# Raw query blocks as pairs of 1024 columns, feed-forward work in half units and new hand-written orders in a fused attention and feed-forward kernel

## The chip, the cores and the metric

The kernel runs on one core of a Trainium2 chip. The metric is the device time of one execution in microseconds (us); here three runs are shown. A second number is the span of one profiled execution, from its first to its last instruction. The engines have short names in what follows: PE (TensorE, matrix multiplications), DVE (VectorE), ACT (ScalarE), POOL (GpSimd) and SP (SyncE, which here only issues transfers). PSUM is the accumulator memory, eight banks of 512 f32 columns on 128 partitions.

## The reference

```python
# S = 2048 tokens, D = 448, H = 16 heads of 28, F = 1792, all float32
g = sigmoid((x * gate_w).sum(-1, keepdims=True))
qkv = (x @ wqkv).reshape(B, S, 3, H, 28)
p = softmax(q @ k.T * 28 ** -0.5)          # per head
a = (p @ v) @ wo
gate = x @ W_gate
h = gate * (gate > 0) * (x @ W_up)
b = h @ W_down
out = g * a + (1 - g) * b
```

## The kernel before

There are three phases. The first, up to about 140 us, makes Q, K and V with three-pass high and low products and writes Q and K to DRAM (`qk_d`). The last, from 1017 us, is the down projection and the output projection. Between them lie **32 rounds**. Round r works on head h = r // 2 and on eight of its sixteen key tiles, against all 2048 queries, which are four blocks of 512 (0 to 3).

What PE, ACT and DVE issue inside a round, and in which order, is written out by hand in the list of strings `ROUNDS`, one string per round. A letter is one piece of work, and the digit behind it is the PSUM bank it uses:

- **m**: a row maximum (`smax`). PE multiplies 128 queries by 512 keys (L288) of a head that comes *later*, and DVE reduces the bank to one column (L290). When all maxima of a head are there, `smax_end` writes the maxima as extra rows of that head's Q, so that scores come out already lessened by the maximum. The list `MAXIMA` runs over the heads in order, so an m belongs to whichever head is next in that list, wherever it stands.
- **s**: a score tile (`scores`). PE multiplies 128 keys by 512 queries (L315), and ACT writes its exponential to SBUF (L317).
- **r, d, e**: the *raw* way, for a query block without row maxima. PE makes a raw score tile for the next round (`raw_scores`, L323), ACT copies it to SBUF (L327), DVE keeps a running maximum (`raw_max`, d, L330). At the end of the round `raw_top` reduces that maximum over the partitions with transposes and reductions (L340 to L353), sends the row to DRAM (`mr_d`, L354) and broadcasts it back (L357) into the one tile `top`. In the next round POOL subtracts it from each raw tile (`raw_less`, L361), and ACT takes the exponential (e, `raw_exp`, L365).
- **x**: one pass of the feed-forward gate and up products (`gu_mm`, L701). A unit has two halves of ten passes and one last pass with 64 rows; the last passes of the two halves run side by side on the two halves of PE's rows.

Before the change, block 3 goes the raw way in every round from the third, and block 2 too where `WIDE` or `BOTH` name the head; a head then has 16, 12 or 8 rows of tiles with maxima (`rows_of`, `parts_of`).

A round ends with the last feed-forward passes, `raw_exp` for what is left, `relu`, in odd rounds the loads of head h + 3's K (`load_k`, four transfers), then `raw_top`, the products `gate * up` (`spill_h`), Q (`load_q`, four transfers and a fifth from `z_d`), the next feed-forward weights (`next_w`) and last `pv`: 64 matmuls of the probabilities by V (L739). Nearly all transfers are issued on SP, one behind the other in program order; where SP waits for a transfer's input or for its buffer, those behind it wait too. K and Q have three buffers each (`h % 3`), so head h + 3 overwrites head h, whose last scores are in round 2h + 1. The maxima of head h + 3 are the first to use the new data.

Of the kernel before, what the change touches and what calls it, by code (L numbers as in the profile page):

```python
# [9 lines left out]
F32 = mybir.dt.float32  # L10
# [9 lines left out]
P = 128  # L20
S = 2048
D = 448
H = 16
# [26 lines left out]
    ("m2m3m6m7s0s1uxxxxs0xm2lxs1xm3xxs6s2xm0m7xUxxxm3m6xs2m0s7m1xxs3m2xxm7xm1m0s3s2xxm7xxm1s0xxm3m7xm1s2m0xs3xxxxm"  # L50
     "2m3xs1xm0xm2xs3xm1xm0xx"),
    ("xxr2s1m0xm3s7r6m2xxs1s3s7dm0xr2dxxxs6s1xm0s3s7xr2xm6s0xds3xs7xm6s1r2m3xs7xs6dm1r0xr3xxdm7s2s1xdxs0xs2m7s1s3x"
     "xxs2m7s0r1m3xs2xxxxdm3s0s2xxxxxs0xs3m2s1xxs0xs3s2m1"),
    ("xxr6m2r1m0xs3r7xxs2r6xxds0xr1dxs2ds7xdr3m0xs6m2xs1m7dxs0xs2m6m1s7xs0r3m2s6dxs7xxs1m2s0m6xm7r3xs1s0dxm2xxm1m7"
     "xs3xxm0s2s1xm3s7exm2s0m1xexem3xm2xxm0exm3exxm2xs1m0xxem3xm1s2m0"),
    ("xxs0m2s1m7s6xxm0s3m2r1xr7m6s0dxs2m3s1xm6s0m7r2xdr1s3xm0s6xxexds7r3m2m0s6xxs7r1xdm2s0s6xdm7s3xs2m0s1m6xs3m7s2"
     "s0m1xr6m3r7es2xs1ds0d"),
    ("xxr2m0m6r1m3r7r2xdxs1r0xs6ddxxr3m1xr7xds6xm2s0xs1dr3xm6s0em2xxr7xs6dm1xs2m0s3xds6s1m2xs3xm0s6s7m2m1xr3xs0xxd"
     "s7xs2m1r0dxs7m3s2xs1xxs7m0s2r3m1xexxdr2s0xxdxr1xxxdem3r0xdxr2dxs1"),
    ("xxs0xm7xs1m2xs3m6m7xs1s0m3xs2m6s7xxm0m1xm2s7xr6m3xs1m7s0xm2xs1s3xs7m6r2m1xs3xem0m7xxxr1xr0s3xxr7dxds2xxr1edd"  # L60
     "xxdr3xr0dxxexexxm1eedxxxxem3xm1em2x"),
    ("xs7r0r2m6s1xm7dr3xs0xm6xdr1s7m0dxr2xds6xr3xr7dxs1s0s6xxds2xm1s3xxs6m0s2m1m3s7s6xm2s0xm1s7s3m6xs2m0s1s7m3xs6m"
     "2s1em0exm3r7s6m2s1m0d"),
    ("xxm7s1r2m0r6m3xr1xm7s0xds2m3xs6xm7s1s2m0s3m6xs7m1r2m0xr3xs7xddr1xdxs0m7r6xs2s3dr0m1xs7xm2xr6ds3xxs7xdr1m2ds3"
     "s0xxm7exxs2m3s0r1m7xds2xm3r0xs7xm2s1xxr3dxdxr1s2xm0exxxr3exxr0ds2dxdx"),
    ("xxs2m7r1m0s6xr3m2s1s7m0r6xm3dr2xxds0s1m7xr3xs6xds1xm2r7dxr6s0s3xxdxm1exxm0er7m6xs1xds3xs0m2m1s6xr3m7dr0s2xex"
     "xdr1xm7dxexxr0m3r2xedxxer1xxr3xxr0exxxdxxdds2m1xde"),
    ("xxxm0m2r7s1m3xs6xm7r2m0xxdxs3m1xs6xm0m2s3xm7s1xm0r6m3s2xxdxr7m0s2dexr1xm6xs2m0m3s7dxexxs2xs7m0xm3xs1m2s7em0x"
     "xs3m1exm7m2xr0dr3dxxexxxm2r1xxxexm0m3exs2dxxe"),
    ("xxr7m1s0r6m2ds3xm7s1r0xxdr2s3xxds1xr6m7xr0xs1s2dm3xdr7xs1m6xs3xds0s2s1m6xm3s0m7xexs6m2s1m0xs3s7m6m2s1xs3m0s7"  # L70
     "s6m1xs2m3r0m7s6dm1s2e"),
    ("xxs2m0s7m1r3xm6s2m0xs7xr3m1s6m2xxs7m3r0m6s1xr2dxs7s3s6ds1xxm0xm2s7m3s6xr0m1s2m7s6s3xxs1dm2xxs6m3s0m1s2r7m6xs"
     "3xdm1xs2xr0m3r7dxxr1xxds3r2dxm0xs7dxr3r1dxxr0xr2xddexxxxedr1m3dxr0xxdxe"),
# [24 lines left out]
    ("xxr7m6r1r0xxr2xr1xs3r6ddxdxr0dr7xr2xs3xdxdr6xxr0xr1dxdr3xdds2xs7s6xxdm0s2s1m7m3exxs2m0m1r7xexxs2ds3m0xxxm1es"
     "2m7s3m0xexr1m2s3xdexxs0xm2s3exm1exm0xr3em2dxxxs1m0"),
    ("xxs0m2s7m1r3m6xs0m2xr1m7s3xm0s6m2r1r7xxdr6xs0ds3r2dxxxm7ds0xs1r6m3xs0dxr2m1ds7xs3xr0m6s1xxr2xr3dxedxxr1s0xr7"  # L100
     "xxdxes3dxdr0m1ds2xxxexm3xxm1er2m0dexm3exxr1xexxdm0ex"),
    ("xxr7m2s0m6r1m3xs7m2s0r6m1dxs7s3xm0s2xm1r7dxs3r6xr0m2xs1s3ds7dxxem2xr6m1xr3m7dxs0xdr1s2xxs7dr0xxxs2dxs7r1exm3"
     "s2xxm7r0dxdexm3exxxexr1xm2r0ddxxr3dxxexr2xdexexxm1"),
    ("xxxm0m2r7s1m3xs6xm7r2m0xxdxs3m1xs6xm0m2s3xm7s1xm0r6m3s2xxdxr7m0s2dexr1xm6xs2m0m3s7dxexxs2xs7m0xm3xs1m2s7em0x"
     "xs3m1exm7m2xr0dr3dxxexxxm2r1xxxexm0m3exs2dxxe"),
    ("xs7m2s1m6xr3s0m7s1m2xs3m6m0xs7m2r1xs3dm6xs7r0xm2s3xxdm7m1es6xr3xs0m2s6xr7xdm1s0s2xdr6m3xs1xds2m7s0xs3m1s6m2x"
     "s0m7s3xm1s6s2m0xr7m3dr6s1em2m0d"),
    ("xxs2r7s1s0xr3xdxs2s7xr6s0s1dxxs3r2xds0s7xs6r3s1xxs7xds2s0xr1s6s3xs2dxs7xs6r0s3r1dxxs7ds2exs6e"),
    ("xs7s2s0r1xr6s7xs2dxr1s0s3xs7xdxs2r0s6s3dxs7s1xr2s6xds3xxr0r1xdexxdxes6s3xs2xxs6s7s3xs0r1s2s6d"),
    ("xxs1xs0xs2s3s6xxxxs1s2s7xxs0xs6xxxxs7s1xs3xxs2s0xxxxxes2xs1s7xexes2exxs1xs3xxxs0xxxxxexexxs1s2"),  # L110
]

WIDE = (2, 4, 6, 8, 10, 12, 13)

BOTH = (4, 6, 8, 10, 12, 13)

# [12 lines left out]
def gated_mix_kernel(ctx, tc, x, wq, wo, wgu, wd, out):  # L129
# [17 lines left out]
    banks = [psum.tile([P, TB], F32, name=f"b_{k}") for k in range(8)]  # L147
# [80 lines left out]
    def raw_js(r):  # L228

        return [] if r < 2 else [3, 2] if r // 2 in (WIDE if r % 2 else BOTH) else [3]  # L230

    def raws(r):
        return [(i, j) for i in range(8 * r, 8 * r + 8) for j in raw_js(r)] if r < 2 * H else []

    def prob(i, j):
        r, k = divmod(i, 8)
        if j == 3 or j in raw_js(r):
            if j == 3 and r % 2 == 0:
                return slot(k)[:, 3]
            if j == 2 and r % 2 and r // 2 in BOTH:  # L240
                return slot(k)[:, 2]
            return V.rearrange("p g h k d -> p (g h k d)")[:, (k + 8 * (3 - j)) * TB:(k + 8 * (3 - j) + 1) * TB]
        return slot(k)[:, j]
# [4 lines left out]
    def top(a, n=1):  # L248
        return slot(8)[:, 2 + a:2 + a + n].rearrange("p a t -> p (a t)")
# [23 lines left out]
    def rows_of(h):  # L273

        return NK if h == 0 else NK - 8 if h in BOTH else NK - 4

    def parts_of(h, u):
        return 2 if h in WIDE and u > 7 else 4

    MAXIMA = [(h, u, c) for h in range(H) for u in range(rows_of(h)) for c in range(parts_of(h, u))]  # L280

    def smax(k, ps):
# [3 lines left out]
        if u == 0 and c == 0:  # L286
            MX[h] = keep.tile([P, 4 * n], F32, name=f"mx_{h}", tag="mx", bufs=2)
        nc.tensor.matmul(ps, Q[h][:, u * P:(u + 1) * P], K[h % 3][:, c * TB:(c + 1) * TB], start=True, stop=True)  # L288
        at = 4 * u + c - (2 * (u - 8) if parts_of(h, u) == 2 else 0)
        nc.vector.tensor_reduce(MX[h][:, at:at + 1], ps, axis=AX.X, op=OP.max)  # L290
        if u == n - 1 and c == parts_of(h, u) - 1:
            M[h] = keep.tile([P, n], F32, name=f"m_{h}", tag="m", bufs=2)
# [39 lines left out]
    def raw_top(r):  # L332
# [6 lines left out]
        for a in range(n):  # L339
            nc.vector.transpose(run(a), run(a))  # L340
# [763 lines left out]
```

## Time and profile before

| | |
|---|---|
| time, three runs | 1196.99, 1204.61, 1202.27 us, median 1202.27 |
| span of the profiled execution | 1198.7 us (its own time is not given) |
| first phase | 0 to about 140 us |
| rounds 0 to 31 | about 140 to 1017 us |
| last phase | 1017 to 1199 us |
| busy share of the span | PE 99%, DVE 75%, ACT 70%, POOL 52% |

The end of a round is the end of its `pv` block on PE: round 7 at 365.4, round 8 at 396.3, round 10 at 448.5, round 11 at 479.3, round 12 at 507.3, round 16 at 618.2, round 17 at 646.2, round 23 at 811.7, round 24 at 845.4. In the profile a line such as L288 is a line of the kernel; "b" is a PSUM bank, "P" and "V" hold probability tiles, "mx" the columns of maxima. A timeline row gives the start, the length and the instruction, and in brackets how long the engine had been idle ahead of it and what released it.

### The profile page before, as it was taken

How to read it: one execution, taken by the hardware profiler on the slowest of the kernel's cores; microseconds unless marked ns; L12 is line 12 of the kernel's file. 1: busy time of each engine (PE TensorE's matmuls, PEld its weight loads, DVE VectorE, ACT ScalarE, POOL GpSimd, SP SyncE). 2: the span in 40 equal slices, each digit the busy share in tenths (PEclk: the TensorE clock that was granted, in tenths of full speed). 3: DMA queues.
4: the chain of work that ended last, by engine and by line, in shares of the span. 5: the costliest groups of instructions: out<-in, count | busy, mean ns of one | idle time of the engine just before them, and what ended most of it. 6: DMA issues, size and time to landing. Idle time of an engine off the chain costs nothing. (4 is left out here: it accounts for less than half of the span.)

```text
span 1198.7 us, 18744 instructions
## 1 busy us (share of the span) xinstructions
PE 1186.6 (99%) x6343; PEld 858.2 (72%) x6343; DVE 900.3 (75%) x1579; ACT 839.4 (70%) x1671; POOL 627.4 (52%) x631
## 2 busy tenths in 40 slices
PE   9999999999999999999999999998999999999998
PEld 6888866666576666667666766666666666989998
DVE  5498777888788879888898889887888872553342
ACT  5311668798998888888888888986998886532121
POOL 4332325566875864776388557657688474100000
PEclk9999999999999999999999999999999999999999
DMA  8956755363646361644554253625452452743432
GB/s 295 340 211 243 264 183 184 114 208 97 211 142 217 128 198 55 191 122 166 182 176 159 68 169 119 200 88 179 149 178 81 160 150 84 232 147 115 132 115 83
DMA packets 68936, 195.89 MB, mean 163 GB/s; under 512 B 15170, under 2 KB 21858, under 8 KB 64414
## 3 DMA queue, kind: packets, MB, share of 16 engines
q1 hardware_dynamic: 55896, 148.72, 38.8%
q0 software_dynamic: 12512, 45.51, 10.7%
q8 instruction: 50, 0.82, 0.3%
q10 hardware_dynamic: 432, 0.46, 0.1%
q14 instruction: 46, 0.38, 0.1%
HBM read 133.99 MB, written 61.12 MB: 163 GB/s over the span
## 5 line engine op out<-in xcount | busy, mean ns | idle before, releaser
L290 DVE TENSOR_REDUCE mx<-b 128x1 f32<-128x512 f32 x680 | 441.6, 686 | 48.8 <-PE b L288 46.0
L317 ACT ACTIVATE P<-b 128x512 f32<-128x512 f32 x672 | 373.7, 633 | 65.5 <-PE b L315 62.8
L701 PE MATMUL b<-X,wg 128*128 128x512 f32 (+1 forms) x1232 | 394.1, 399 | 1.9 <-DMA wg<-wgs_d 1.6
L701 PEld LDWEIGHTS b<-X,wg 128*128 128x128 f32 (+1 forms) x1232 | 217.5, 188 | 69.4 <-issue 20.9
L288 PE MATMUL b<-K,Q 128*128 128x512 f32 x680 | 257.4, 392 | 3.8 <-DMA Q<-z_d 2.0
L315 PE MATMUL b<-Q,K 128*128 128x512 f32 x680 | 247.8, 391 | 0.0
L361 POOL TENSOR_TENSOR V<-V,P 128x512 f32<-128x512 f32 x176 | 224.8, 1294 | 32.9 <-DMA P<-mr_d 27.9
L361 POOL TENSOR_TENSOR P<-P,P 128x512 f32<-128x512 f32 x168 | 214.9, 1294 | 28.9 <-DMA P<-mr_d 15.6
L739 PE MATMUL b<-P,v 128*32 128x512 f32 x1680 | 228.5, 594 | 0.0
L330 DVE TENSOR_TENSOR P<-b,P 128x512 f32<-128x512 f32 x279 | 186.3, 684 | 12.9 <-ACT P L327 6.7
L739 PEld LDWEIGHTS b<-P,v 128*32 128x32 f32 x1680 | 68.4, 110 | 132.1 <-issue 111.8
L739 PE MATMUL b<-V,v 128*32 128x512 f32 x368 | 156.0, 594 | 0.8 <-ACT V L365 0.8
L288 PEld LDWEIGHTS b<-K,Q 128*128 128x128 f32 x680 | 127.9, 188 | 32.1 <-issue 2.4
L315 PEld LDWEIGHTS b<-Q,K 128*128 128x128 f32 x680 | 127.7, 188 | 29.6 <-ACT P L317 2.0
L1009 PE MATMUL b<-WD,hh 128*128 128x448 f32 x672 | 138.2, 366 | 0.3
L1009 PEld LDWEIGHTS b<-WD,hh 128*128 128x128 f32 x672 | 126.1, 188 | 10.9 <-DVE WD L186 0.5
L323 PE MATMUL b<-Q,K 128*128 128x512 f32 x344 | 131.8, 391 | 0.0
L327 ACT ACTIVATE V<-b 128x512 f32<-128x512 f32 x168 | 104.3, 635 | 24.0 <-PE b L323 23.5
L365 ACT ACTIVATE V<-V 128x512 f32<-128x512 f32 x176 | 110.6, 670 | 3.6 <-POOL V L361 3.5
L180 ACT ACTIVATE hh<-hr 128x512 fp32r<-128x512 f32 x52 | 32.8, 631 | 109.3 <-PE b L1009 109.3
L365 ACT ACTIVATE P<-P 128x512 f32<-128x512 f32 x168 | 105.5, 679 | 2.6 <-POOL P L361 2.6
L327 ACT ACTIVATE P<-b 128x512 f32<-128x512 f32 x160 | 98.5, 625 | 8.5 <-PE b L323 7.3
(102 smaller groups left out, 1039.7 us busy)
## 6 DMA issues: line engine op xcount, KB each, us to landing
wg<-wgs_d SPq DMA_DIRECT2D x42, 896.0 KB
Q<-qk_d SPq DMA_DIRECT2D x64, 224.0 KB
h_d<-rl POOLq DMA_DIRECT2D x56, 256.0 KB, 3.5
hr<-h_d SPq DMA_DIRECT2D x52, 256.0 KB
wgs_d<-wg SPq DMA_DIRECT2D x14, 896.0 KB
K<-qk_d SPq DMA_DIRECT2D x52, 224.0 KB
qk_d<-st POOLq DMA_DIRECT2D x21, 512.0 KB, 4.9
wgr<-wgu SPq DMA_DIRECT2D x13, 512.0 KB
```

What stands on the lines that cost most here:

```text
L288: nc.tensor.matmul(ps, Q[h][:, u * P:(u + 1) * P], K[h % 3][:, c * TB:(c + 1) * TB], start=True, stop=True)
L290: nc.vector.tensor_reduce(MX[h][:, at:at + 1], ps, axis=AX.X, op=OP.max)
L315: nc.tensor.matmul(ps, K[h % 3][:, kt * P:(kt + 1) * P], Q[h][:, j * TB:(j + 1) * TB], start=True, stop=True)
L317: nc.scalar.activation(prob(i, j), ps, AF.Exp, scale=SCALE)
L323: nc.tensor.matmul(ps, K[h % 3][:, kt * P:(kt + 1) * P], Q[h][:, j * TB:(j + 1) * TB], start=True, stop=True)
L327: nc.scalar.activation(own, ps, AF.Copy)
L330: nc.vector.tensor_tensor(run(3 - j), ps, run(3 - j) if i % 8 > 1 else prob(i - 1, j), op=OP.max)
L361: nc.gpsimd.tensor_tensor(own, own, top(3 - j), op=OP.subtract)
L365: nc.scalar.activation(own, own, AF.Exp, scale=SCALE)
L701: nc.tensor.matmul(ps, WS[i][rows, s, a], xf(i // NF, b)[rows], start=(n == 0), stop=(n == NT - 1))
L739: nc.tensor.matmul(po[32 * j:32 * j + 32], VH[h][:, i % NK], prob(i, j), start=(i == i0), stop=(i == i0 + ni - 1))
L1009: nc.tensor.matmul(ACC[i // NF][t][:, :D], HH[i][:, a, t * P:(t + 1) * P], WD[:, f, b], start=(f == 0 and n == 0), stop=(f == NF - 1 and n ...
```

## The change

It does the following.

- Query blocks 2 and 3 both go the raw way in every round from the third. They are handled as one tile of 1024 columns: two matmuls into two neighbouring banks, then one ACT copy, one running maximum, one POOL subtraction and one exponential of 1024 columns each.
- Head 0 keeps 16 rows of tiles with maxima, and each later head has 8 with four columns: 544 row maxima in all, where there were 680.
- PSUM becomes one tile of eight banks, so that a pair of banks can be read by one instruction.
- Feed-forward work is dealt out in half units: a round holds three halves (18 rounds) or four, so a unit can end in the next round. There are 1100 x letters as before. `gu_mm` still pairs the last passes by lanes, where both halves stand in one round.
- A new letter T places `raw_top` inside the order; 23 rounds have it (not 0, 1, 4, 10, 11, 14, 18, 28 and 31). There `raw_top`, with its two transfers, comes ahead of `load_k`.
- All 32 orders are new. Round 1 has no m; rounds 2 to 27 have 16 on average.
- Smaller: the raw copies of round 1 go to DVE instead of those of rounds 29 and 30; `relu` goes to DVE from round 29; V has one buffer, loaded in the head's own first round, at the sixth s; `rl` has three buffers; `load_k` is always on SP.

The core of the diff:

```diff
-WIDE = (2, 4, 6, 8, 10, 12, 13)
-
-BOTH = (4, 6, 8, 10, 12, 13)
+PASSES = 10
...
-    banks = [psum.tile([P, TB], F32, name=f"b_{k}") for k in range(8)]
+    whole = psum.tile([P, 8, TB], F32, name="b")
+    pairs = [whole[:, k:k + 2] for k in range(0, 8, 2)]
+    banks = [whole[:, k] for k in range(8)]
...
     def raws(r):
-        return [(i, j) for i in range(8 * r, 8 * r + 8) for j in raw_js(r)] if r < 2 * H else []
+        return range(8 * r, 8 * r + 8) if 2 <= r < 2 * H else []
...
     def rows_of(h):
-        return NK if h == 0 else NK - 8 if h in BOTH else NK - 4
+        return NK if h == 0 else NK - 8
...
-    def raw_scores(i, j, ps, late=False):
+    def raw_scores(i, b, late):
...
+        for j in (2, 3):
+            nc.tensor.matmul(banks[b + j - 2], K[h % 3][:, kt * P:(kt + 1) * P], Q[h][:, j * TB:(j + 1) * TB], start=True,
+                             stop=True)
+        ps = pairs[b // 2].rearrange("p a t -> p (a t)")
         if late:
-            nc.vector.tensor_copy(own, ps)
+            nc.vector.tensor_copy(prob_pair(i), ps)
         else:
-            nc.scalar.activation(own, ps, AF.Copy)
...
+    def raw_max(i, b):
+        nc.vector.tensor_tensor(run(0, 2), pairs[b // 2].rearrange("p a t -> p (a t)"),
+                                run(0, 2) if i % 8 > 1 else prob_pair(i - 1), op=OP.max)
...
+    def raw_less(i):
+        own = prob_pair(i)
+        nc.gpsimd.tensor_tensor(own, own, top(), op=OP.subtract)
...
+    HALVES = [order.count("x") // PASSES for order in ROUNDS] + [0]
+    done = sum(HALVES) // 2
...
+            elif o == "T":
+                assert not new and not tops
+                raw_top(r + 1)
+                topped = True
...
         if r % 2 and h + 3 < H:
-            load_k(h + 3, nc.gpsimd if nxt % NF == 0 else nc.sync)
+            load_k(h + 3)
         if r % 2 == 0:
             next_w()
-        if raws(r + 1) and r:
+        if not topped:
             raw_top(r + 1)
```

What this does to the order on the engines shows at three places. First, SP in the odd round 17, before: its K, Q and z loads (K_175 and Q_178 are head 11's buffers) and `raw_top`'s two transfers (`mr_d_103`, and the broadcast into P_1499).

```order
L373 DMA f_d_125<-rows_179 32x32
L376 DMA fa_5626<-f_d_125 32x512 x2
L260 DMA K_175<-qk_d 28x2048 x4
L354 DMA mr_d_103<-rows_179 16x32
L357 DMA P_1499<-mr_d_103 128x512
L266 DMA Q_178<-qk_d 28x2048 x4
L269 DMA Q_178<-z_d 2x2048
L690 DMA wg_1241<-wgs_d_138 128x1792
```

The same place on SP after the change (K_168 and Q_171 are head 11's buffers now).

```order
L358 DMA f_d_118<-rows_172 32x32
L361 DMA fa_5151<-f_d_118 32x512 x2
L340 DMA mr_d_96<-rows_172 32x32
L343 DMA P_1500<-mr_d_96 128x1024
L254 DMA K_168<-qk_d 28x2048 x4
L260 DMA Q_171<-qk_d 28x2048 x4
L263 DMA Q_171<-z_d 2x2048
L676 DMA wg_1238<-wgs_d_129 128x1792
```

`mr_d` and the broadcast moved ahead of the four K loads, which stood ahead of them before; Q follows K directly.

Second, PE at the start of round 18, behind round 17's last `pv` matmul, before: L288 is a row maximum, L315 a score, L323 a raw score, L701 a feed-forward pass. K_174 and Q_177 belong to head 10, loaded in round 15; the first use of head 11's K_175 and Q_178 stands some 40 matmuls further on.

```order
L739 MATMUL b_72<-V,v_4904 32x512
L701 MATMUL b_73<-X_166,wg_3081 128x512 x2
L323 MATMUL b_76<-Q_176,K_173 128x512
L288 MATMUL b_70<-K_174,Q_177 128x512
L315 MATMUL b_69<-Q_176,K_173 128x512
L323 MATMUL b_75<-Q_176,K_173 128x512
L288 MATMUL b_71<-K_174,Q_177 128x512
```

After the change (L725 is `pv`, L288 the transpose of head 10's finished maxima, L279 a row maximum, L302 a score):

```order
L725 MATMUL b<-V,v_4957 32x512 x2
L288 MATMUL b<-ident,m_5300 8x128
L279 MATMUL b<-K_168,Q_171 128x512
L302 MATMUL b<-Q_169,K_166 128x512
L279 MATMUL b<-K_168,Q_171 128x512
L302 MATMUL b<-Q_169,K_166 128x512
L279 MATMUL b<-K_168,Q_171 128x512
```

The first maximum of the round now uses head 11's K_168 and Q_171, which SP loads in round 17; the same holds for the first maximum of each even round from 2 to 26.

Third, DVE at the end of round 17 after the change: the last maxima, running maxima (L319) and the pieces of `raw_top` (L328 to L336).

```order
L319 TENSOR_TENSOR P_1500<-b,P_1500 128x1024
L280 TENSOR_REDUCE mx_4917<-b 128x1 x2
L319 TENSOR_TENSOR P_1500<-b,P_1500 128x1024
L328 STREAM_TRANSPOSE P_1500<-P_1500 128x512 x2
L331 TENSOR_REDUCE best_of<-P_1500 128x32
L325 TENSOR_REDUCE P_1500<-best_of 32x32 x4
L334 TENSOR_REDUCE P_1500<-P_1500 32x32
L336 STREAM_TRANSPOSE rows_172<-P_1500 32x32
L280 TENSOR_REDUCE mx_4917<-b 128x1 x2
L283 TENSOR_REDUCE m_5300<-mx_4917 128x8
```

Two row maxima and their final reduction (L283) stand behind `raw_top` now; before, `raw_top` stood behind all of the round's maxima, as the last work of DVE ahead of the feed-forward products.

More of the change, by code (lines that the diff above doesn't have):

```diff
@@ L56 @@
[L56 to L61, printed above, removed]
@@ L660, in gated_mix_kernel @@
     WSB = [fe.tile([P, 2, 7, P], F32R, name=f"wg_{k}") for k in range(2)]
-    done = sum(order.count("x") for order in ROUNDS) // 20
+    HALVES = [order.count("x") // PASSES for order in ROUNDS] + [0]
+    done = sum(HALVES) // 2
     def lane(k):
@@ L878, in gated_mix_kernel @@
                 keep_w(1)
[L879 to L880 removed]
+        assert not todo and not mine and not rest and not new, r
+        gone = made
         for i, half, ps in units:
             gu_mm(ps, i, half, NT - 1)
[L883 to L884 removed]
+        if exps:
+            raw_exp(exps.pop(0))
         for i, half, ps in units:
```

251 lines of the change are left out of this document (118 added, 133 removed).

## Prediction

> **What bounds the kernel now.** I began with the busy shares and the clock of the page.
>
> ```profile
> span 1198.7 us, 18744 instructions
> PE 1186.6 (99%) x6343; PEld 858.2 (72%) x6343; DVE 900.3 (75%) x1579; ACT 839.4 (70%) x1671; POOL 627.4 (52%) x631
> PEclk9999999999999999999999999999999999999999
> ```
>
> PE is busy for 99% of the span at full clock, so each matmul that goes is worth its slot, and each stall that comes costs all of its length. No other engine has more than 75%. Next I cut the rounds out of the span (windows view: window, its length, then busy us and instructions of each engine, the granted clock, DMA share and GB/s). The rows are rounds 8, 11 and 24, and the rest of round 24 after its stalls.
>
> ```profile
> 365.40:396.30 30.90, 29.24 (x163) 18.74 (x156) 25.20 (x45) 25.59 (x50) 21.94 (x20) 1.00 0.59 194
> 479.30:507.30 28.00, 28.00 (x164) 18.70 (x156) 25.05 (x45) 25.12 (x50) 21.80 (x20) 1.00 0.60 188
> 811.70:845.40 33.70, 30.06 (x164) 19.73 (x156) 25.14 (x45) 25.58 (x50) 20.89 (x18) 0.95 0.51 170
> 826.30:845.40 19.10, 18.96 (x112) 11.63 (x112) 14.76 (x28) 15.05 (x29) 13.31 (x12) 0.91 0.22 73
> ```
>
> Round 11 is the plain case: 28.00 us, PE never idle. Rounds 24 and 8 run the same work in 33.70 and 30.90 us: 5.7 and 2.9 us of stall and slow clock. What happened in round 24 stands in PE's timeline (start, length, instruction, and in brackets the idle time ahead of it and who ended it).
>
> ```profile
> 818.97 0.39 PE L323 MATMUL b<-Q,K 128*128 128x512 f32 x1
> 819.19 0.39 PE L701 MATMUL b<-X,wg 128*128 128x512 f32 x1
> 819.42 0.39 PE L323 MATMUL b<-Q,K 128*128 128x512 f32 x1
> ...
> 823.40 0.47 PE L288 MATMUL b<-K,Q 128*128 128x512 f32 x1 [2.01 <-DMA Q<-z_d]
> ...
> 826.43 1.07 PE L701 MATMUL b<-X,wg 128*128 128x512 f32 x2 [1.64 <-DMA wg<-wgs_d]
> ```
>
> Consecutive 512-column matmuls start 0.227 us apart (818.97, 819.19, 819.42): that is the slot I price with. And the first row-maximum matmul of a new head (L288) stood still for the last piece of that head's Q. The transfer queue of SP shows why, in round 17 (nothing stalled behind it) and in round 23, ahead of the stall.
>
> ```profile
> 638.75 3.14 SPq L260 DMA_DIRECT2D K<-qk_d  x4
> 642.77 0.31 SPq L354 DMA_DIRECT2D mr_d<-rows  x1
> 645.97 0.35 SPq L357 DMA_DIRECT2D P<-mr_d  x1
> 646.38 3.10 SPq L266 DMA_DIRECT2D Q<-qk_d  x4
> ...
> 809.38 0.32 SPq L354 DMA_DIRECT2D mr_d<-rows  x1
> 815.43 0.32 SPq L357 DMA_DIRECT2D P<-mr_d  x1
> 815.80 3.15 SPq L266 DMA_DIRECT2D Q<-qk_d  x4
> 818.99 0.42 SPq L269 DMA_DIRECT2D Q<-z_d  x1
> ```
>
> Every odd round loads one head's K (L260) and Q (L266, L269). K goes out first; then come the two transfers of `raw_top`, `mr_d` and the broadcast of the running maximum (`top`, L357), which has to wait until `mr_d` has landed; only then Q. In round 17 the broadcast left 3.20 us after `mr_d`, in round 23 6.05 us. Q's first load left at 815.80 and PE was released at 823.40: **7.6 us** from the first Q load to a usable head. Round 17 ended at 646.2, so Q is never there at the start of the even round. Before, that costs nothing in most rounds, because the orders put 5 to 15 maxima of the older head ahead of it: the new head's first matmul stands 39 or more places into the even round.
>
> **The change part by part.** First PE's own work. Of 680 row-maximum matmuls 136 go; scores and raw scores together stay at 1008; feed-forward passes stay at 1100.
>
> - 136 x 0.227 = **-30.9 us**.
> - Half units: 18 rounds now have three instead of four, and a third half has no lane partner for its last pass: nine more slots, 9 x 0.227 = **+2.0 us**.
> - The stalls of rounds 8 and 24 belong to orders that are gone: **-8.6 us** (bounds 0 and -12, since the other rounds hold some 3 us more that their matmul counts do not explain).
>
> ```profile
> 838.97 7.00 PE b L739 x64
> ```
>
> This row of the chain of waits gives the probabilities-times-V block that closes a round. A round with four halves has 32 scores, 16 maxima, 40 passes and 2 slots of last passes: 90 x 0.227 + 7.0 + about 0.5 at the edges = 27.9, and round 11 shows 28.00. With three halves it is 80 slots: **25.7 us**. That is the time the other engines get per round.
>
> Second, those engines, by groups (line, engine, tiles and shapes, count, busy us, mean ns, idle before) and by pieces of their timelines.
>
> ```profile
> L290 DVE TENSOR_REDUCE mx<-b 128x1 f32<-128x512 f32 x680 | 441.6, 686 | 48.8 <-PE b L288 46.0
> L361 POOL TENSOR_TENSOR V<-V,P 128x512 f32<-128x512 f32 x176 | 224.8, 1294 | 32.9 <-DMA P<-mr_d 27.9 <-DMA o_d<-os 5.1
> L330 DVE TENSOR_TENSOR P<-b,P 128x512 f32<-128x512 f32 x279 | 186.3, 684 | 12.9 <-ACT P L327 6.7 <-ACT V L327 3.6
> 485.81 1.29 POOL L361 TENSOR_TENSOR V<-V,P 128x512 f32<-128x512 f32 x1
> 487.07 1.28 POOL L361 TENSOR_TENSOR P<-P,P 128x512 f32<-128x512 f32 x1
> 612.10 1.30 DVE L340 STREAM_TRANSPOSE P<-P 128x512 f32<-128x512 f32 x2
> 613.43 1.22 DVE L343 TENSOR_REDUCE best_of<-P 128x32 f32<-128x1024 f32 x1
> 616.11 0.21 DVE L353 TENSOR_REDUCE best_of<-rows 32x32 f32<-32x64 f32 x1
> 957.59 9.95 ACT L317 ACTIVATE P<-b 128x512 f32<-128x512 f32 x20 [0.18 <-PE b L315]
> 16.88 1.06 ACT L180 ACTIVATE X<-xr 128x1024 fp32r<-128x1024 f32 x1 [2.56 <-DMA xr<-x]
> ```
>
> DVE per round: 16 maxima at no more than 0.69, seven running maxima of 1024 columns at 1.22 (the 1024-column reduction; two of 0.684 are the upper end), and `raw_top`, 612.10 to 616.3, 4.2: 11.0 + 8.5 + 4.2 = 23.7. ACT: 16 exponentials at 0.50 (20 in 9.95), eight copies and eight exponentials of 1024 columns at 1.06: 8.0 + 17.0 = 25.0 with little else, close to 25.7 and no more than round 11 held. POOL: eight subtractions of 1024 columns; no row has that size, two of 512 are 2.59 and consecutive starts are 1.26 apart, so 2.4 to 2.6 each, 19.4 to 20.7 a round. All three fit beside PE, barely, and I price them at nothing in rounds 2 to 30. In round 31, with 58 slots and so 20.7 us of PE work, POOL's 19.4 and the last exponential of 1.06 end behind PE's start on the last V tiles: **+3 us** (0 to 5). The 1024-column tile, the single V buffer and `raw_top`'s extra columns lie beside PE too; without that cover a round would take the longest of these sums, ACT's 25.0.
>
> Third, and this decides: **what the new orders do to a head's first use.** After the change each head has 32 maxima and rounds 2 to 27 hold 16 a round on average, but round 1 has none, so the lead is gone. In all 13 even rounds from 2 to 26 the first maximum of the round belongs to the head that was loaded in the round just before, and it is among the first five matmuls. PE runs its list in order, so scores, feed-forward and everything else queue behind it, and ACT, DVE and POOL run dry. On SP's queue the odd rounds now have `mr_d` and the broadcast first, then all four K loads, then Q: `raw_top` has moved ahead of K where the order holds a T (all odd rounds from 3 to 27 but 11); in 1 and 11 Q still stands behind it.
>
> ```profile
> SPq L357 <- DMA mr_d<-rows: 39.9, 15, 7.3
> PE b L288 <- DMA Q<-z_d: 2.0, 1, 2.0
> ```
>
> The waits view (total us, times, longest) has the broadcast at 39.9 us in 15 waits, 2.7 each, and a single stall of PE for Q. Now the time line in an odd round of 25.7 us. The broadcast overwrites the one `top` slot, so POOL's eighth subtraction must be done: 19.4 us after it began, 0 to 2.5 us into the round, so at 21.9 at the latest by that. `mr_d` left 3.4 us ahead of the end of round 17 and `raw_top` now stands two or three us earlier, at about 20.7; with round 17's 3.20 the broadcast goes out at 23.9. I take the middle, 22.9. K's first load follows 0.4 us behind (645.97 to 646.38), its four take 3.1, so Q's first leaves at 26.4 and all is landed 7.6 us later, at **34.0**. PE wants it at 25.7 plus three slots, **26.4**. Stall: **7.6 us**, bounds 5.0 (the broadcast out at 21.0 and a landing 0.7 us quicker) and 9.5 (the broadcast at 24, and K's four loads sharing the bandwidth that Q had alone).
>
> Behind the stall the clock: after stalls of 2.0 and 1.6 us round 24 ran 19.10 us at 0.91, which is 19.10 x 0.09 = **1.7 us** lost. I add it each time (bounds 0 and 2.5). 13 x (7.6 + 1.7) = **+120.9**.
>
> Sum: -30.9 + 2.0 - 8.6 + 3.0 + 120.9 = +86.4, so a span of 1285.1. The profiled execution's own time is not given; its span stands 3.6 below the median of 1202.27, and I add these back: 1288.7, said as **1288**.
>
> Two pages speak on this. The Trainium skill, TensorE: Matmul & The Clock Gate, What's actually happening, lets the clock fall to half only after an idle window of some 3.4 us and gives it back after as long a busy one: a stall of 7.6 us would then cost about 1.7 us more (an estimate from that page), the same sum, though in round 24 the clock fell after two stalls that were each shorter. The Trainium skill, DMA: Bandwidth & Descriptors, Anatomy of one DMA, gives a transfer about 2.0 us of fixed cost besides its bytes (fitted on GpSimd's path): with the last piece issued at 29.9 a head would be there at about 32, a stall of 5.5 and a time near 1261. The row of 7.6 us speaks against it.
>
> **The rivals.** *The loads are hidden* and PE's saving comes through: without the last term the sum is -34.5, which gives **1168**, or 1176 if rounds 8 and 24 keep their losses. For it: PE is the bound today, and only one Q wait cost anything. It decides below 34.5 / 13 = 2.7 us of stall and clock per even round. Against it: a head would have to be there 2.7 us behind PE's want at 26.4, hence by 29.1, when the Q loads alone would still be going out on SP. *The `top` slot becomes a loop*: the next broadcast waits for eight subtractions, and the next subtraction for the broadcast.
>
> ```profile
> L361 POOL TENSOR_TENSOR P<-P,P x8: 1258/1282/1303, 819.4 to 836.8; 128x512 f32<-128x512 f32 x8
> ```
>
> POOL's first subtraction (819.4, the row gives the first and last start) came 4.0 us behind the broadcast's issue at 815.43. With 20.7 for eight, 4.0, and 2.7 of waiting for `mr_d` the loop is 27.4 us against 25.7: 26 x 1.7 = +44 without a stall for Q, and with -34.5 of the other terms this gives +10, **1212**, no change. For it: no row has a 1024-column subtraction, and from 2.6 us each on this case is over 1% slower. Against it: `mr_d` would have landed before POOL is done. *ACT becomes the bound* at 25.0 plus its waits, up to 27: 26 x 1.3 = +34, **1202**, no change; against it, ACT holds 25.1 of 28.00 now without holding PE up. *One tile of eight banks ties all matmuls to all readers*, so the change doesn't give single banks: PE would wait about one reader per matmul, hundreds of us; the waits in the program name one bank's reader each, and I give it 0.01, inside slower.
>
> **How the numbers follow.** Stalls for new heads 0.77, nearly all of it between 1232 (5.0 us, no clock loss: 65 - 34.5 = +30) and 1324 (12.0 us: 156 - 34.5 = +121); `top` loop 0.08; hidden 0.09; ACT 0.05; banks 0.01. Range 1210 to 1325: it takes in the loop and leaves out hidden, ACT and what lies beyond 1325. Faster by over 1% 0.09, within 1% (about what a measurement of this kernel can tell) 0.10, slower 0.81.
>
> **What would show it.** In the waits of PE, the row for the maxima (L279 now) waiting for Q or `z_d` some 13 times, 5 to 9 us each, some 100 us in all; odd rounds near 25.7 us and even rounds near 35; a granted clock of about 0.9 behind each stall; in SP's queue `mr_d`, broadcast, K, Q in odd rounds. POOL's subtraction at 2.4 to 2.6 us and `raw_top` at 4.2. I am wrong if K and Q leave SP by some 18 us into the odd round, if PE's waits for Q stay below 30 us in all, or if POOL or ACT, not a transfer, ends PE's longest waits.

## The result and the profile after

The changed kernel takes **1397.59 us** (median of four runs, 1396.66 to 1399.38) against 1202.41: ratio 1.162, 95% interval 1.160 to 1.165. The forecast was 1288, and the range ended at 1325. The direction and the place were right, the size was 110 us short. The busy shares, the clock and two groups of the page after:

```profile
span 1394.9 us, 17848 instructions
PE 1225.6 (88%) x6207; PEld 834.0 (60%) x6207; DVE 898.8 (64%) x1346; ACT 880.6 (63%) x1346; POOL 752.3 (54%) x515
PEclk9999999898989898999898999999998999999999
...
L319 DVE TENSOR_TENSOR P<-b,P 128x1024 f32<-128x1024 f32 x195 | 238.4, 1223 | 100.8 <-ACT P L316 55.6
L347 POOL TENSOR_TENSOR V<-V,P 128x1024 f32<-128x1024 f32 x120 | 283.5, 2403 | 26.6 <-DMA P<-mr_d 21.5
```

PE issues 136 matmuls fewer, as counted (6343 - 6207), and yet is busy longer: part of its work runs at a lower clock, and where the clock is full its matmuls still start further apart (round 19 below is busy for 27.45 us with work for 25.7). The sizes priced by neighbours came out as expected, 1.22 us for the running maximum of 1024 columns and 2.40 for POOL's subtraction. Rounds 19 and 20 and some of the 2 us slices that follow the end of round 19 (windows view, columns as before):

```profile
798.70:827.35 28.65, 27.45 (x147) 16.26 (x147) 23.86 (x36) 24.11 (x34) 21.30 (x11) 1.00 0.28 89
827.35:869.75 42.40, 31.93 (x159) 20.40 (x158) 24.46 (x37) 25.71 (x36) 22.40 (x14) 0.88 0.37 120
...
828.00:830.00 2.00, 0.03 (x1) 0.00 (x0) 0.18 (x1) 1.11 (x2) 1.46 (x3) 1.00 0.90 260
834.00:836.00 2.00, 0.00 (x0) 0.00 (x0) 0.00 (x0) 0.00 (x0) 2.00 (x2) 0.50 1.00 285
838.00:840.00 2.00, 2.00 (x7) 1.52 (x6) 1.29 (x2) 0.65 (x1) 2.00 (x2) 0.50 0.92 369
```

From 828 to 836 PE stands still, and DVE and ACT soon run dry too. The transfer engines are at 0.90 to 1.00 in these slices, and the granted clock falls to 0.50 while PE waits. PE's waits of the whole kernel:

```profile
PE b L279 <- DMA wg<-wgs_d: 47.1, 5, 10.5
PE b L279 <- DMA Q<-mh: 29.4, 3, 11.1
PE b L279 <- DMA Q<-z_d: 18.1, 2, 9.2
PE b L310 <- DVE P L319: 16.3, 37, 0.8
PE b L279 <- DMA Q<-qk_d: 15.1, 2, 8.7
PE b L279 <- DMA v<-v_d: 13.2, 1, 13.2
PE b L279 <- DVE P L319: 9.4, 26, 0.7
PE b L302 <- DVE P L319: 9.2, 21, 0.7
```

Five rows are the first row maximum (L279) waiting for transfers: 5 + 3 + 2 + 2 + 1 = **13 waits, 122.9 us**, where before there was one of 2.0. Some rows name weights, `mh` or V, but the matmul reads only K and Q, and the view only infers the releaser. In round 20 it names the weights, yet when PE began at 837.27 only 109 of the 256 packets (7 KB each) of the two weight blocks had ended, so neither block had landed. The last 8 KB packet of K, Q and `z_d` ended at 836.00, and in all 13 rounds PE began 0.9 to 1.5 us behind that packet. Three rows are a second kind: **84 short waits, 34.9 us, for banks that DVE's running maximum (L319) still reads.** Before, PE had no such row of any size. SP's queue and PE around the same place:

```profile
822.36 0.30 SPq L340 DMA_DIRECT2D mr_d<-rows  x1
823.72 0.34 SPq L343 DMA_DIRECT2D P<-mr_d  x1
824.15 3.15 SPq L254 DMA_DIRECT2D K<-qk_d  x4
827.35 3.06 SPq L260 DMA_DIRECT2D Q<-qk_d  x4
830.45 0.43 SPq L263 DMA_DIRECT2D Q<-z_d  x1
...
827.32 0.71 PE L310 MATMUL b<-Q,K 128*128 128x512 f32 x2
837.27 1.19 PE L279 MATMUL b<-K,Q 128*128 128x512 f32 x2 [9.24 <-DMA wg<-wgs_d]
843.37 0.40 PE L279 MATMUL b<-K,Q 128*128 128x512 f32 x1
843.60 0.39 PE L302 MATMUL b<-Q,K 128*128 128x512 f32 x1
```

K leaves 3.2 us before round 19 ends and Q at its end, behind the broadcast, as forecast. The head is usable 9.9 us after Q's first load, not 7.6. Then PE runs at half speed: from 837.27 to 843.37 it issues 14 matmuls in 6.1 us, 0.43 apart in place of 0.227, so 2.9 us are lost. At 843.60 the distance is 0.23 again. Round 20 is the worst case but not the rule. Here are the 8 us behind PE's restart in rounds 14 and 20, with the granted clock third from the end:

```profile
618.36:626.36 8.00, 8.00 (x29) 6.53 (x30) 6.15 (x9) 5.38 (x9) 8.00 (x5) 0.80 0.13 49
837.27:845.27 8.00, 8.00 (x23) 6.34 (x24) 5.20 (x8) 4.46 (x7) 8.00 (x4) 0.62 0.38 151
```

That is 8.00 x 0.20 = 1.6 us lost in round 14 and 3.0 in round 20. The same windows in all 13 rounds lose 1.6 to 3.0 us, 2.3 on average and **30 us** in all.

### The profile page after: what moved, and what is told of

It reads as the page before. It is cut to its first block, busy times and chain, and to the rows that moved or that the text cites. A ratio compares the mean times of both kernels' runs of the same rounds, so it can differ in the third digit from the quotient of the medians.

```text
span 1394.9 us, 17848 instructions
## 1 busy us (share of the span) xinstructions
PE 1225.6 (88%) x6207; PEld 834.0 (60%) x6207; DVE 898.8 (64%) x1346; ACT 880.6 (63%) x1346; POOL 752.3 (54%) x515
## 5 line engine op out<-in xcount | busy, mean ns | idle before, releaser
L280 DVE TENSOR_REDUCE mx<-b 128x1 f32<-128x512 f32 x544 | 350.5, 681 | 162.9 <-PE b L279 162.3
L304 ACT ACTIVATE P<-b 128x512 f32<-128x512 f32 x528 | 297.1, 600 | 173.1 <-PE b L302 165.7
L279 PE MATMUL b<-K,Q 128*128 128x512 f32 x544 | 221.8, 430 | 133.5 <-DMA wg<-wgs_d 47.1
L319 DVE TENSOR_TENSOR P<-b,P 128x1024 f32<-128x1024 f32 x195 | 238.4, 1223 | 100.8 <-ACT P L316 55.6
L347 POOL TENSOR_TENSOR V<-V,P 128x1024 f32<-128x1024 f32 x120 | 283.5, 2403 | 26.6 <-DMA P<-mr_d 21.5
L347 POOL TENSOR_TENSOR P<-P,P 128x1024 f32<-128x1024 f32 x120 | 280.6, 2368 | 4.1 <-DMA P<-mr_d 4.0
L725 PE MATMUL b<-P,v 128*32 128x512 f32 x1536 | 226.1, 594 | 0.0
L302 PE MATMUL b<-Q,K 128*128 128x512 f32 x544 | 213.5, 416 | 9.6 <-DVE P L319 9.2
L279 PEld LDWEIGHTS b<-K,Q 128*128 128x128 f32 x544 | 108.6, 202 | 179.2 <-issue 106.5
L316 ACT ACTIVATE V<-b 128x1024 f32<-128x1024 f32 x120 | 122.4, 1031 | 75.3 <-PE b L310 74.5
L725 PEld LDWEIGHTS b<-P,v 128*32 128x32 f32 x1536 | 60.3, 110 | 145.3 <-issue 139.2
L302 PEld LDWEIGHTS b<-Q,K 128*128 128x128 f32 x544 | 105.9, 197 | 57.7 <-DVE P L319 25.1
L316 ACT ACTIVATE P<-b 128x1024 f32<-128x1024 f32 x112 | 114.0, 1029 | 18.6 <-PE b L310 17.7
L310 PEld LDWEIGHTS b<-Q,K 128*128 128x128 f32 x480 | 88.4, 197 | 60.8 <-DVE P L319 40.6
L351 ACT ACTIVATE P<-P 128x1024 f32<-128x1024 f32 x120 | 122.0, 1064 | 0.0
L351 ACT ACTIVATE V<-V 128x1024 f32<-128x1024 f32 x120 | 120.0, 1070 | 2.6 <-POOL V L347 2.6
L725 PE MATMUL b<-V,v 128*32 128x512 f32 x512 | 113.2, 594 | 0.0
```

The source lines that it names most:

```text
L280: nc.vector.tensor_reduce(MX[h][:, 4 * u + c:4 * u + c + 1], ps, axis=AX.X, op=OP.max)
L302: nc.tensor.matmul(ps, K[h % 3][:, kt * P:(kt + 1) * P], Q[h][:, j * TB:(j + 1) * TB], start=True, stop=True)
L304: nc.scalar.activation(prob(i, j), ps, AF.Exp, scale=SCALE)
L310: nc.tensor.matmul(banks[b + j - 2], K[h % 3][:, kt * P:(kt + 1) * P], Q[h][:, j * TB:(j + 1) * TB], start=True, stop=True)
L316: nc.scalar.activation(prob_pair(i), ps, AF.Copy)
L319: nc.vector.tensor_tensor(run(0, 2), pairs[b // 2].rearrange("p a t -> p (a t)"), run(0, 2) if i % 8 > 1 else prob_pair(i - 1), op=OP.max)
```

## The experiments

Two causes stood against each other after the trace: heads that land late (A), and banks that are held too long (B). The first four kernels each touch one.

**Maxima one round later** (`lag`):

```diff
 # ROUNDS[2]
-    "s2m7s0m1s4m6r2m5m7r0xxdxs6r2xxxds5xs7r0dxm6s5xs2xm3m7...eddTxxxm0m1m7"
+    "s2s0s4r2r0xxdxs6r2xxxds5xs7r0dxs5xs2x...eddTxxx"
 # ROUNDS[28]
-    "s7r0xxr2xs5s6xs7dxr0xxdr2xxdxxr6xx..."
+    "s7r0xm6xr2xs5s6m0xs7dxr0m5xxdr2xm0xdxxr6m2xx..."
```

> Edit: the changed kernel with the row maxima one round later; round 2 issues none of its 16, round 28, which had none, issues 16. So the maxima at the start of an even round belong to the head loaded three rounds before, and the first use of a new head stands in the odd round behind it. Nothing else moves. Theory A (a new head's K and Q land late): the 13 stalls at the start of rounds 2 to 26, 124.6 us in all, go, and with them the half-speed stretch behind each, 14 matmuls at 0.43 instead of 0.227 us, 2.9 us each, 38 in all: about 1398 - 163 = 1235 us, granted clock 1.00 in even rounds. Rival (the stalls only shift to the next thing that lands late, the weights or V): PE keeps a wait for a transfer in the even rounds, some 5 us each, and the time stays above 1300. Rival (the slow clock is not the stalls' doing): the stalls go, 1273, and the clock in the even rounds stays below 0.95.

Measured: **1263.42 us**, ratio to before 1.051 (1.047 to 1.054), so 134 less than the changed kernel. Rounds 19, 20 and 28, and PE's longest waits:

```profile
695.35:723.99 28.64, 27.32 (x148) 16.30 (x147) 23.69 (x35) 24.43 (x36) 21.74 (x12) 1.00 0.28 89
723.99:754.35 30.36, 29.10 (x158) 18.33 (x158) 24.27 (x38) 24.72 (x34) 22.25 (x13) 1.00 0.48 165
962.62:1003.08 40.46, 32.51 (x158) 18.14 (x158) 25.01 (x38) 24.95 (x34) 22.18 (x14) 0.96 0.34 112
...
PE b L310 <- DVE P L319: 19.3, 37, 1.4
PE b L279 <- DVE P L319: 12.0, 27, 1.1
PE b L302 <- DVE P L319: 11.5, 23, 1.9
```

Round 20 falls from 42.40 to 30.36, with its clock at 1.00: the stalls and the slow clock go together, and no later transfer takes their place. That settles A and the clock's cause. 28 us of the expected gain are missing. Some 8 are the clock, which had cost 30 us and not the expected 38 (13 times round 20's 2.9); about 11 are in round 28, whose 16 added maxima ask for banks that are in use (40.46, against 26.0 in the changed kernel and 3.6 for 16 slots); some 9 are not placed. The waits for L319 are all still there, and longer: 42.8 us.

**Loads ahead of the maximum's transfers** (`loads_first`):

```diff
                 ns += 1
+                if not mine and r % 2 and h + 3 < H:
+                    load_k(h + 3)
+                    load_q(h + 3)
...
-        if r % 2 and h + 3 < H:
-            load_k(h + 3)
...
-        if r % 2 and h + 3 < H:
-            load_q(h + 3)
```

> Edit: the changed kernel with the four K loads, the four Q loads and z issued right behind the last score of the odd round, ahead of the transfers of raw_top. Theory A as predicted (the order on SP's queue makes the head late): K leaves SP some 5 us earlier, the eight loads go out back to back as before, and the 13 stalls shrink from 9.6 to about 4.5 us each, the clock loss with them by 1 us each: 13 x 6 = 78 us less, about 1320. Rival (the transfers' bandwidth is the limit, not the queue's order: the DMA engines are at 0.9 to 1.0 from 826 to 840 us of the profile): landing moves by less than 2 us, 1370 or more. Rival (the broadcast of the maximum, now last, makes POOL late instead): odd and even rounds get longer at their ends, PE waits for POOL or ACT at the V products, no gain.

Measured: **1313.41 us**, 1.091 (1.089 to 1.094), 84 less than the changed kernel. The kernel holds its own control, since the loads moved ahead of `raw_top` only where the last score stands ahead of T. Below are rounds 10 and 14, SP around round 9's loads and then around round 13's, and PE at the start of round 14.

```profile
429.77:460.19 30.42, 29.07 (x159) 18.32 (x158) 24.19 (x37) 25.36 (x36) 22.21 (x14) 1.00 0.31 101
551.33:593.43 42.10, 31.67 (x159) 20.50 (x158) 24.57 (x37) 25.25 (x36) 22.38 (x14) 0.88 0.37 118
...
419.58 3.06 SPq L260 DMA_DIRECT2D Q<-qk_d  x4
425.64 0.31 SPq L340 DMA_DIRECT2D mr_d<-rows  x1
427.01 0.35 SPq L343 DMA_DIRECT2D P<-mr_d  x1
...
548.02 0.34 SPq L343 DMA_DIRECT2D P<-mr_d  x1
548.45 3.15 SPq L254 DMA_DIRECT2D K<-qk_d  x4
551.65 3.06 SPq L260 DMA_DIRECT2D Q<-qk_d  x4
...
560.49 0.77 PE L279 MATMUL b<-K,Q 128*128 128x512 f32 x1 [8.95 <-DMA Q<-z_d]
```

In round 9 Q left at 419.58, 10 us before the round's end at 429.77, and round 10 has no stall. In round 13 the last score stands behind T; the queue's order is the old one, Q leaves at 551.65, behind the end at 551.33, and the stall is 8.95. So the gain was not 13 stalls cut by half: six are gone whole (rounds 4, 6, 8, 10, 18, 26), two are shorter (2 and 12, whose round before has no T), and five are as they were (14, 16, 20, 22, 24). PE's waits in these seven rounds add up to 53.3 us, and the clock behind them loses 14.5: 85 us less than the 122.9 and 30 before, where the gain is 84. The place of `raw_top` on SP's queue makes the head late in the rounds that have it, which is the mechanism of the forecast.

**The maximum from SBUF** (`max_sbuf`):

```diff
-        nc.vector.tensor_tensor(run(0, 2), pairs[b // 2].rearrange("p a t -> p (a t)"),
+        nc.vector.tensor_tensor(run(0, 2), prob_pair(i),
```

> Edit: the changed kernel with the running maximum taken from the copy of the raw pair in SBUF instead of from the two PSUM banks; so the banks come free behind ACT's copy (1.03 us) and not behind DVE's maximum (1.22 us more). Theory B (a raw pair holds two banks too long, and PE runs into held banks in every round): PE's waits for L319, 35.9 us in 88 waits, go, odd rounds fall from 28.9 towards 25.7 and even ones by about 2: about 1398 - 60 = 1338 us. Rival (rounds without a stall are longer because ACT or DVE cannot keep up): the waits only change their name, to ACT's copy, and the time stays within 10 us of 1398; or DVE's maximum gets slower when both operands lie in SBUF.

Measured: **1588.82 us**, 1.320 (1.317 to 1.323), 191 *more* than the changed kernel. By groups and shapes:

```profile
L347 POOL TENSOR_TENSOR V<-V,P 128x1024 f32<-128x1024 f32 x120 | 360.7, 3041 | 28.8 <-DMA P<-mr_d 22.0 <-ACT P L304 3.4 <-ACT P L316 3.3
L319 DVE TENSOR_TENSOR P<-P,P 128x1024 f32<-128x1024 f32 x105 | 260.5, 2481 | 36.3 <-ACT P L316 32.5
L319 DVE TENSOR_TENSOR P<-V,P 128x1024 f32<-128x1024 f32 x90 | 141.6, 1573 | 33.9 <-ACT V L316 30.7
L319 DVE TENSOR_TENSOR P<-V 128x1024 f32<-128x1024 f32 x15 | 78.1, 5204 | 18.2 <-ACT V L316 18.2
```

With both operands in SBUF, DVE's maximum takes 2.48, 1.57 or 5.20 us on average instead of 1.22, and POOL's subtraction of V tiles 3.04 instead of 2.40. It answers nothing on B, since it swapped one cost for a larger one.

**One PSUM tile alone** (`before_whole`):

```diff
-    banks = [psum.tile([P, TB], F32, name=f"b_{k}") for k in range(8)]
+    whole = psum.tile([P, 8, TB], F32, name="b")
+    banks = [whole[:, k] for k in range(8)]
```

> Edit: the kernel before, with PSUM as one tile of eight banks and nothing else. Theory: waits are kept for each bank, so nothing changes: 1202 us within 0.5%. Rival (one tile ties the banks together): every matmul waits for the readers of other banks, and the time is at least 1300 us; a part of the loss of the changed kernel would then come from here.

Measured: 1203.96 us, 0.9993 (0.9977 to 1.0009). The tile costs nothing by itself.

For B two kernels followed, both on `lag`, where no stall covers the short waits. **A thin maximum** (`lag_thin`) and **copies and maxima of 512 columns** (`lag_split`):

```diff
 # lag_thin
+        n = 2 * TB if i % 8 == 1 else 32
+        nc.vector.tensor_tensor(run(0, 2)[:, :n], pairs[b // 2].rearrange(...)[:, :n], ...[:, :n], op=OP.max)
 # lag_split
+        for j in (2, 3):
+            nc.scalar.activation(prob(i, j), banks[b + j - 2], AF.Copy)
...
+        for j in (2, 3):
+            nc.vector.tensor_tensor(run(j - 2), banks[b + j - 2], run(j - 2) if i % 8 > 1 else prob(i - 1, j), op=OP.max)
```

> Edit: on the kernel with the maxima one round later, the running maximum reads all 1024 columns only for the first pair of a round and 32 columns for the other six (the maximum over the keys is so left out for most columns); DVE then holds a raw pair's banks for about 0.1 us instead of 1.22. Theory B (PE runs into banks that DVE's maximum holds, 44 us of PE's waits for L319 and a slow slot behind each): the waits go, odd rounds fall from 28.7 to about 26, and the time from 1263 by 60 to 75 us to about 1195. Rival (ACT, 24.3 us busy in a round of 28.7, cannot keep up and DVE is only named because it comes last): the waits change to ACT's copy and exponentials, the time falls by less than 20 us. Rival (DVE's total work is too much, not the holding): DVE's work falls by 6.7 us a round and the gain would be the same as by theory B; the next run, which keeps the work, tells these apart.

> Edit: on the kernel with the maxima one round later, a raw pair is copied by ACT and reduced by DVE as two instructions of 512 columns each instead of one of 1024; POOL's subtraction and the exponential stay pairs. The work is the same plus one more instruction's fixed cost for each (about 0.1 us: 0.50 for 512 against 1.03 for 1024 on ACT, 0.61 to 0.68 against 1.22 on DVE). Theory B: the first bank of a pair comes free about 1.1 us earlier and DVE can begin while ACT copies the second half, so half of the wait goes: some 25 to 40 us less than 1263, about 1230. Rival (ACT is short of time): ACT's extra fixed cost of some 0.8 us a round makes it 1263 or up to 20 us longer.

Measured: `lag_thin` **1200.96 us** (62 less than `lag`), `lag_split` **1216.68** (47 less; ratio to before 1.010, 1.008 to 1.011). Round 19 of `lag_thin` and of `lag_split`, and the first row on DVE's maximum in PE's waits of `lag_split`:

```profile
664.74:690.37 25.63, 25.63 (x147) 16.77 (x147) 17.70 (x35) 23.70 (x36) 21.75 (x12) 1.00 0.27 88
673.10:700.05 26.95, 26.79 (x147) 16.39 (x147) 23.98 (x42) 24.57 (x44) 21.82 (x12) 1.00 0.32 90
...
PE b L302 <- DVE P L320: 1.9, 2, 1.4
```

Without the holding, round 19 takes 25.63 us: the 25.7 of the matmul count. With the same work in halves it takes 26.95, while ACT and DVE are busy as long as in `lag` (24.57 and 23.98 against 24.43 and 23.69). So for these 47 us it is not the amount of work but how long one instruction keeps a bank from PE; the gain from splitting was larger than the 25 to 40 us expected. For the other 16 us of `lag_thin` the two runs don't tell a shorter hold from less work: there DVE is busy for only 17.70 us in round 19. `lag_thin` is a measurement and no candidate, since it leaves most of the maximum out.

**The split without the lag** (`after_split`) asks whether the two causes add.

> Edit: the changed kernel with the raw pairs copied and reduced as two instructions of 512 columns, and nothing else; the maxima stand as in the changed kernel, so the new heads are late as before. If the two causes add up (late heads 134 us, banks held by the 1024-column copy and maximum 47 us), this is 1398 - 47 = 1351 us, and PE still shows 13 waits of some 9 to 10 us at the start of the even rounds. Rival (they hide each other: in the even rounds PE's stall already gives DVE and ACT time to free the banks): only the odd rounds gain, 13 x 1.9 = 25 us, about 1373.

Measured: **1348.70 us** (1.121, 1.119 to 1.124), 49 less than the changed kernel, against 47 on top of `lag`. PE still has its 13 waits for a new head, 125.7 us in all (122.9 before), and no row for DVE's maximum. The two causes add.

Three versions then used both findings (`orders2`, `orders3`, `orders4`; `orders5` is a variant): 512-column copies and maxima, eight maxima of round 2 moved to round 28, the letters of rounds 2 to 30 in another sequence with other banks. The core of it, with round 28's string for one:

```diff
-    "s7r0xxr2xs5s6xs7dxr0xxdr2xxdxxr6xxs0s1dxxr2x..."
+    "s7s1s5m0r6xr2m5xdxxs6xxxr0xdxxxs6m3xs2s7xm6xr0xx..."
...
-                if ns == 8 and r % 2 == 0 and h:
+                if ns == (8 if r == 30 else 12) and r % 2 == 0 and h:   # orders4; 12 alone in orders2 and orders3
```

> A version built on both findings: 512-column copies and maxima; 8 of round 2's 16 maxima dropped there and 8 issued in round 28, so that the first 8 maxima of an even round belong to the older head and the new head's first stands some 48 matmuls, 11 us, into the round; the letters of rounds 2 to 30 put into another sequence with other banks, chosen so that a bank is asked for only some 2 us after its last use; the reciprocal of the row sums at the 12th score of an even round instead of the 8th. Same instructions otherwise. If late heads and held banks are the two causes and there is no third, rounds come near their matmul counts (25.7 us with three halves, 28.0 with four) and the time falls below both kernels, 1170 to 1185 us. Rival (the loop of the one top slot, eight subtractions of 2.4 and about 6 us of broadcast, sets 26 to 27 us a round): odd rounds stay above 26.4 and POOL's subtractions wait for nothing but the broadcast; about 1190 to 1200.

> As orders3, with another such sequence found for the same rules; it tells whether a gain belongs to the rules or to one lucky order. Expected within 8 us of orders3. If the two differ by more, the banks' waits depend on more than the distance to a bank's last use.

Measured: `orders3` 1206.24 us (1.003, 1.002 to 1.004), `orders2` 1201.54 (1.000, 0.998 to 1.002): within 8 us of each other, but above the 1170 to 1185 that I expected. In `orders2` the last round took 27.0 us, and POOL's timeline showed why:

```profile
994.48 1.28 POOL L752 TENSOR_TENSOR os<-os,rb 128x512 f32<-128x512 f32 x1 [7.74 <-DMA rb<-l_d]
```

The later reciprocal made POOL stand for the row sums with the last round's eight subtractions behind it.

> As orders2, with the reciprocal of the row sums back at the 8th score in round 30 alone. In orders2 the last round took 27.0 us against 20.7 of PE work: POOL stood 7.7 us for the row sums of head 14 (transfer rb), and its eight subtractions for the last round began that much late. Expected: the wait goes, round 31 falls to about 23 us, the time from 1201.5 to about 1197, 0.4% below the kernel before. Rival (the broadcast of the maximum is not there earlier either): no change.

> As orders4, with relu on DVE instead of ACT in rounds 2 to 8, where ACT also splits the feed-forward weights and rounds take 28 us against 26.5 later. If ACT's time is what those rounds wait for, they lose about 0.6 to 1.2 us each: about 1191. Rival (DVE is as short there): no change or up to 5 us longer.

Measured: `orders4` **1196.30 us**, 0.994 (0.992 to 0.996); `orders5` 1196.87, 0.994 (0.991 to 0.996). `orders4` beats both kernels, the one before by 0.6%. Its rounds 19, 20 and 31:

```profile
664.61:691.23 26.62, 26.60 (x147) 16.23 (x147) 24.24 (x42) 24.89 (x44) 21.71 (x13) 1.00 0.34 127
691.23:719.87 28.64, 28.50 (x159) 18.41 (x158) 24.96 (x45) 25.09 (x42) 22.25 (x14) 1.00 0.55 180
988.63:1011.29 22.66, 22.17 (x126) 12.65 (x125) 3.17 (x5) 15.94 (x25) 21.00 (x11) 1.00 0.29 114
```

PE is busy nearly throughout, but these rounds still stand 0.6 to 0.9 us above their matmul counts. The rival of the `top` loop said that odd rounds would stay above 26.4, and they do (26.62); but round 19 of `lag_thin`, with the same eight subtractions and the same broadcast, took 25.63, so the loop doesn't hold a round at 26.4. What stretches these rounds stays open.

Rounds 3 to 8 take about 28 us where their count is 25.7, some 14 us too long together. Rounds 4 and 5 of `orders4`, then of `orders5`, which has `relu` on DVE there (fourth and fifth pair of columns: ACT and POOL):

```profile
248.58:276.60 28.02, 27.50 (x145) 16.05 (x145) 24.84 (x46) 27.76 (x53) 24.85 (x18) 1.00 0.57 205
276.60:304.95 28.35, 27.89 (x148) 16.51 (x147) 23.68 (x42) 25.71 (x46) 27.05 (x19) 1.00 0.35 113
249.35:276.42 27.07, 26.96 (x146) 16.09 (x145) 24.76 (x45) 26.31 (x49) 23.94 (x16) 1.00 0.64 224
276.42:305.42 29.00, 27.89 (x148) 16.53 (x147) 25.41 (x45) 25.73 (x47) 28.09 (x21) 1.00 0.31 103
```

In rounds 3 to 7 ACT and POOL also split the feed-forward weights into high and low parts. ACT is busy for 27.76 of round 4's 28.02 us, more than PE's count; without `relu` it falls to 26.31, and the round falls with it to 27.07 (6 and 8 fall by as much). So ACT's time set round 4. In round 5 POOL is the busiest of the others, and in `orders5` it rises to 28.09 while the round rises to 29.00 (3 and 7: 28.5 and 28.8), so nothing is gained. That POOL sets the odd rounds is likely but not tested.

## Why the prediction was right and wrong

**Right.** The point of decision was the new head's first use, and both halves of it held: 13 stalls, one at the start of each even round from 2 to 26, and the queue's order as the cause (`loads_first`, rounds 10 and 14). Moving the use by a round took 134 us off. The hidden loads (1168) and the tie of all banks (`before_whole`) fell, and so did the `top` loop: POOL's 2.40 us lay in the bounds, and PE's waits have no row of it. ACT as the bound of all rounds fell with round 19 of `lag_thin`, where ACT has the same work and PE meets its count; in rounds 3 to 8 it is another matter (below).

**Wrong: the step that priced the other engines at nothing.** I wrote that the sums of DVE (23.7), ACT (25.0) and POOL (19.4 to 20.7) all fit beside PE's 25.7, "barely", and took that for no cost. The busy sums were about right from round 9 on (23.86, 24.11 and 21.30 in round 19), but a busy sum says nothing of how long PE must stay out of a bank. A raw pair takes two of eight banks, feed-forward sums take three or four to the end of the round, and ACT's copy (1.03) and DVE's maximum (1.22) run one after the other. That is some 2.3 us for two banks at once, where the kernel before needed 1.3 for one (a copy of 0.63, a maximum of 0.68). Price: 62 us by `lag_thin`, of which the split gives back 47 to 49. I had named the 1024-column tile only as work beside PE.

The sums themselves left something out as well: the splitting of the feed-forward weights, here from the end of round 2 to round 7. Round 5 of the changed kernel:

```profile
299.62:329.08 29.46, 27.34 (x147) 16.37 (x146) 23.76 (x36) 26.99 (x43) 27.08 (x19) 1.00 0.31 101
```

ACT is busy for 26.99 us and POOL for 27.08, where I had 25.0 and at most 20.7. Both are more than PE's 25.7, so in such a round they don't fit beside it even as sums.

**Two terms too small, but inside their bounds.** The stalls were 122.9 us, 9.45 each, instead of 13 x 7.6 = 98.8: I took the landing of Q alone from round 24 and put the sharing with K only into the upper bound (9.5), but eight loads, the broadcast and two weight blocks were in flight together (0.90 to 1.00 of the transfer engines). The clock cost 2.3 us a stall instead of 1.7 (bound 2.5): I took the loss from two short stalls. By the Trainium skill's page TensorE: Matmul & The Clock Gate, What's actually happening, the clock would have been back after some 3.4 us of work. In the 13 rounds it took 3.1 to 6.1, 4.6 on average, so the measurement decides. With both terms as measured the forecast would have been about 1321, still inside the range; what put the time outside it is the step above.

**One reading was wrong.** I called the 2.9 us of round 8 before the change stall and slow clock. Its row shows a clock of 1.00 and 1.66 us without PE; the rest lies inside PE's busy time.

Put together: -37.5 + 122.9 + 30 + 62 + 1 (round 31 took 21.6, not 20.7) = +178 on the span, where the trace has 1394.9 - 1198.7 = +196. Some 18 us stay without a name, and some 7 more because that much of the 62 was gained in `lag`'s long round 28 (40.46, in `lag_thin` 33.08), which the changed kernel doesn't have. The sums of rounds 3 to 8 belong to this rest; how much of it they are, no run shows.

## What to carry to other kernels

When work is removed from a list that several streams share, look at what the rest of that list now meets first: a lead that hid a load can vanish with work that looked superfluous. On a kernel bound by the matrix engine, a wider instruction that reads accumulator banks must be priced by the time it keeps the banks, and its followers in the same chain with it, not by its own busy time. A price taken from one round, such as the 2.9 us of clock in round 20, should be read off all the rounds before it is multiplied. A queue that one instruction blocks should be read in the order of issue, with each load set against the matmul that needs it first.

## What the runs showed of the hardware that I had not expected

Behind the 13 stalls PE ran at half speed for 3.1 to 6.1 us of issued work (14 matmuls at 0.43 us in round 20), and the clock fell 1.7 to 5.1 us after the last matmul. In the trace's record of the granted clock the stretches at half speed, from fall to return, are 6.8, 10.2, 13.7 or 17.1 us long, all whole multiples of 3.41. So what a stall lost behind it did not follow from its own length: 2.0 us behind the shortest of 6.42, 1.6 behind one of 8.65, 3.0 behind one of 9.24.

DVE and POOL hinder each other when DVE's two operands both lie in SBUF, and only when they run at the same time. In `max_sbuf` 91 of the 210 maxima had no subtraction of POOL beside them; their median was 1.23 us, as with one operand in PSUM. Of the 119 others the median was 3.05 us and the longest 10.69, and POOL's subtraction took up to 3.46 us instead of 2.40. The Trainium skill, SBUF — State Buffer, Who interferes with whom, has a DVE instruction with two SBUF inputs contend with a GpSimd instruction that reads SBUF. The trace agrees: 1.23 us without such a neighbour, 3.05 with one.
